# Moving the gates' products of a MoE routing to GpSimd, and its exponentials into one activation

## The chip, the cores and the metric

The kernel runs on one core of one Trainium2 chip. The metric is the device time of one execution in microseconds; the kernel before takes 953.64 us in the median of three runs (951.24 to 955.93). Engines are named as in the profile: PE is TensorE (products; PEld its weight loads), DVE is VectorE, ACT is ScalarE, POOL is GpSimd, and SP issues most DMAs.

## The reference

Three stages follow each other. A delta rule runs over 768 positions of 4 x 8 heads of width 48; its outputs are rows of 384 for 3072 tokens. A mixture of 8 experts sends each token to the expert with the largest logit and multiplies by that token's probability (the gate). A dense block of width 2048 with an ELU ends it.

```python
def _moe_ref(x, expert_emb, tau, w1, w2):
    xn = x / (np.linalg.norm(x, axis=-1, keepdims=True) + 1e-06)
    logits = xn @ en.T / tau
    expert_idx = np.argmax(logits, axis=1)
    probs = np.exp(logits - logits.max(-1, keepdims=True))
    probs /= probs.sum(-1, keepdims=True) + 1e-09
    gate_w = probs[np.arange(N), expert_idx]
    for e in range(E):
        mask = expert_idx == e
        h = np.maximum(x[mask] @ w1[e], 0.0)
        out[mask] = gate_w[mask, None] * (h @ w2[e])
```

Since the largest shifted logit is 0, the gate of a token is 1 over the sum of its exponentials. A positive factor passes through the maximum with zero, so the kernel multiplies the token's row of x by it before the expert.

## The kernel before

**Stages.** The attention stage (up to some 357 us) handles the positions in 12 chunks of 64, each for all heads in two halves. The MoE stage and the dense block come after it and hold most of TensorE's work; they need the routing's tables, which `finish_routing` makes from all routings.

**A pair of chunks needs an inversion.** `invert` builds the inverse T of a small triangular system in 30 steps on GpSimd (L1369: a product into tmp, a subtraction from T, with sizes that grow to 128x128 and shrink again to 128x30). VectorE then transposes T into tile a (L1374, twice), four DMAs carry a into bdT, and TensorE multiplies residuals (rh) by bdT in the recurrence of the next pair. The inversion's steps for one pair run while the recurrence of the pair before it is under way.

**The recurrence.** Its products are on TensorE (L1223). Residuals R are turned into rh by ScalarE (L1100) or VectorE (L1101, L1432), states into Sc (L1470), new values into Zc (L1459); block-diagonal copies bdS, bdZ, bdK, bdKT are made by an engine (L1219, L1220) or by DMA.

**Rows for the MoE.** After each chunk, `to_rows` brings the outputs into token rows (L1519), copies them into one of four slots of tile xt (L1529), the logits' parts into lgp (L1531), and sums the squares into ss (L1533, L1534). Slots are used again by the next pair of chunks; a copy into a slot waits until that slot's scatter has landed.

**A routing.** `route` runs after chunks 1, 3, 5, 7 and 9 for the four tiles in xt (routings 1 to 5 below), and after chunks 10 and 11 for two tiles each. It finds the maximum, each token's place in its expert's queue (di), and the inverse norm rn; then per tile an exponential with scale rn and a sum into gs (L339, on ScalarE); then 1/gs on VectorE (L341, L342); then per tile the gate, a product of 128x384 by a column of gs, on ScalarE (L354) or VectorE (L355); then per tile the scatter, an indirect DMA that GpSimd issues (L348) behind a memset of a single element (L347). After the four scatters GpSimd adds 128 to the tokens' numbers (L359), which waits until all four have landed.

**What sets the order.** In the attention stage nothing is scheduled when the kernel is built: the table `STARTS` holds a due time (units of 10 ns) for every operation, all operations are sorted by it, and each engine gets its own in that order. The table `WAYS` says which engine does an operation that could run on several; its entry "gate" has a digit for each of the 24 gates. Each engine works off its instructions in order; one that waits for a semaphore holds up all behind it on that engine.

## Time and profile before

| | |
|---|---|
| median of 3 runs | 953.64 us (951.24 to 955.93) |
| profiled execution | 954.83 us, span 953.4 us |
| mean granted clock of TensorE over the span | 0.971 |
| PE busy over the span | 834.9 us (88%) |
| DVE | 768.4 us (81%) |
| ACT | 600.4 us (63%) |
| POOL | 464.6 us (49%) |

The page's shares are averages over three stages. The change lies in the attention stage alone, so its windows, its waits and the timelines of single engines around the routings are what to read. A timeline's row gives the start from the beginning of the span, the duration, the engine, the line, the operation with its output and inputs, and in brackets the idle time of the engine just before with what ended it. An engine that sits idle there costs nothing unless a later engine waits for it.

### The profile page before, as it was taken

Reading aid. Unit: us, or ns where it says so; the run is one execution under the profiler, and the core shown is the slowest. Engines: PE = TensorE matmul, PEld = TensorE weight load, DVE = VectorE, ACT = ScalarE, POOL = GpSimd, SP = SyncE. Lnnn points to the kernel's source line nnn. Section 1 sums busy time; section 2 is a strip of 40 time slices with the busy share of each in tenths; the row PEclk is TensorE's granted clock in tenths of the full one; section 3 lists DMA queues with packets and bytes.
Section 4 is the critical chain, followed back from the end, with each engine's and each line's share of the span. In section 5 each row is a group of like instructions: output and inputs, shape, how many; then the busy total and the mean of one; then the engine's idle time right before and its main releaser. Section 6 shows DMA issues by size and latency. Waiting matters only on the chain.

```text
span 953.4 us, 28791 instructions
## 1 busy us (share of the span) xinstructions
PE 834.9 (88%) x11734; PEld 695.9 (73%) x11735; DVE 768.4 (81%) x1563; ACT 600.4 (63%) x1094; POOL 464.6 (49%) x707
## 2 busy tenths in 40 slices
PE   0537888798999877999999999889999999999995
PEld 0426788687888764555556568789999999999995
DVE  6787878778787963988898988998887887787884
ACT  8896779877786954455646636666545455465652
POOL 6564677676776432143433412354345555355452
PEclk9958999999999997999999999999999999999998
DMA  6667865847545418867899263210010100100000
GB/s 207 163 133 204 235 151 114 177 110 136 131 106 140 148 51 267 174 226 196 238 251 212 92 119 98 84 51 18 1 51 18 51 19 18 35 18 18 18 18 18
DMA packets 115365, 107.58 MB, mean 113 GB/s; under 512 B 72889, under 2 KB 100317, under 8 KB 114973
## 3 DMA queue, kind: packets, MB, share of 16 engines
q1 hardware_dynamic: 108649, 82.98, 35.8%
q0 software_dynamic: 6080, 22.05, 7.5%
q8 instruction: 93, 1.52, 0.7%
q10 hardware_dynamic: 500, 0.68, 0.3%
q14 instruction: 43, 0.35, 0.1%
HBM read 74.72 MB, written 19.97 MB: 99 GB/s over the span
## 4 chain that ended last, share of the span: by engine, by line
PE 49%; DVE 7%; issue 2%; DMA 2%; ACT 1%; SPq 0%; POOL 0%; POOLq 0%; DVEq 0%; ACTq 0%
PE pa L662 17%; PE acc L682 15%; PE acc L620 8%; PE pa L601 8%; DMA st<-in_w 2%; DVE w L519 1%; DVE wbl L676 1%; DVE w L518 1%; DVE dal L534 1%; DVE hl L615 0%; DVE wal L668 0%; SPq L471 0%; DVE dbl L534 0%; DVE wah L669 0%; PE pa L573 0%
## 5 line engine op out<-in xcount | busy, mean ns | idle before, releaser
L682 PE MATMUL acc<-dbh,wbl 128*128 128x192 f16 x672 | 165.3, 246 | 1.4 <-DVE wbl L676 1.4
L682 PE MATMUL acc<-dbl,wbh 128*128 128x192 f16 x672 | 165.3, 246 | 0.9 <-DVE dbl L534 0.9
L682 PE MATMUL acc<-dbh,wbh 128*128 128x192 f16 x672 | 165.3, 246 | 0.2 <-DVE y L630 0.2
L662 PE MATMUL pa<-x,dah 128*128 128x256 f16 x1152 | 157.3, 273 | 1.8 <-DVE wal L668 1.4
L682 PEld LDWEIGHTS <-wbh 128*128 128x128 f16 x1344 | 121.9, 98 | 1.5 <-issue 0.3
L662 PEld LDWEIGHTS <-dah 128*128 128x128 f16 x1152 | 111.9, 98 | 14.7 <-issue 2.0
L662 PE MATMUL pa<-x,dal 128*128 128x256 f16 x576 | 94.4, 273 | 0.9 <-DVE dal L534 0.9
L601 PE MATMUL pa<-x,wah 128*128 128x440 f16 (+6 forms) x384 | 77.0, 337 | 1.9 <-DVE hl L615 1.8
L1223 PEld LDWEIGHTS <-bdKT 112*128 112x128 f16 x1680 | 58.3, 101 | 21.0 <-ACT bdKT L1219 6.1
L1223 PEld LDWEIGHTS <-bdK 128*128 128x128 f16 x960 | 40.8, 119 | 42.8 <-ACT rh L1100 18.5
L669 POOL TENSOR_TENSOR wal<-wal 128x256 f32<-128x256 f32 (+1 forms) x67 | 44.8, 669 | 54.9 <-DVE wal L668 31.1
L675 ACT CAST wbh<-wal 128x384 f16<-128x384 f32 (+1 forms) x73 | 41.3, 566 | 44.8 <-PE acc L682 20.4
L682 PEld LDWEIGHTS <-wbl 128*128 128x128 f16 x672 | 65.7, 98 | 3.1 <-DVE wbl L676 2.1
L620 PE MATMUL acc<-hh,wbh 128*128 128x440 f16 (+6 forms) x192 | 64.2, 334 | 2.0 <-DVE y L630 1.1
L620 PE MATMUL acc<-hl,wbh 128*128 128x440 f16 (+6 forms) x192 | 64.1, 334 | 1.2 <-DVE hl L615 1.1
L614 ACT ACTIVATE hh<-pa 128x440 f16<-128x440 f32 (+6 forms) x64 | 31.9, 504 | 52.2 <-PE acc L620 24.8
L620 PE MATMUL acc<-hh,wbl 128*128 128x440 f16 (+6 forms) x192 | 64.0, 334 | 0.0
L675 ACT CAST wbh<-wah 128x384 f16<-128x384 f32 (+1 forms) x82 | 46.0, 562 | 25.8 <-DVE wah L668 11.3
L1223 PEld LDWEIGHTS <-bdL 128*128 128x128 f16 x1536 | 52.0, 97 | 13.7 <-issue 7.1
L662 PEld LDWEIGHTS <-dal 128*128 128x128 f16 x576 | 56.4, 98 | 7.7 <-DVE dal L534 1.2
L665 ACT ACTIVATE wah<-pa 128x512 f32<-128x512 f32 x48 | 28.6, 596 | 48.4 <-PE pa L662 28.0
L601 PEld LDWEIGHTS <-wah 128*128 128x128 f16 x384 | 37.3, 98 | 29.8 <-issue 3.6
(317 smaller groups left out, 2390.5 us busy)
## 6 DMA issues: line engine op xcount, KB each, us to landing
st<-in_w SPq DMA_DIRECT2D x24, 512.0 KB
st<-in_w SPq DMA_DIRECT2D x32, 384.0 KB
kraw<-in_k SPq DMA_DIRECT2D x22, 384.0 KB
w<-in_w_in POOLq DMA_DIRECT2D x12, 512.0 KB, 6.3
w<-in_w_out POOLq DMA_DIRECT2D x16, 384.0 KB, 5.9
xs_scratch<-in_zeros SPq DMA_DIRECT2D x8, 675.5 KB
raw<-in_q SPq DMA_DIRECT2D x12, 448.0 KB
vraw<-in_v SPq DMA_DIRECT2D x12, 384.0 KB
```

What stands on the lines that cost most here:

```text
L518: self.dve(n, lambda m=m, hi=hi: v.scalar_tensor_tensor(out=m, in0=hi, scalar=-0x40000000, in1=m, op0=ALU.bitwise_and, op1=ALU.bitwise_or) ...
L519: self.dve(n, lambda m=m, lo=lo: v.scalar_tensor_tensor(out=m, in0=lo, scalar=29, in1=m, op0=ALU.logical_shift_right, op1=ALU.bitwise_or), ...
L534: self.dve(n, lambda f=f, part=part: v.scalar_tensor_tensor(out=part("l"), in0=f, scalar=sc, in1=part("h"), op0=ALU.mult, op1=ALU.subtract ...
L601: self.nc.tensor.matmul(self.pa[i][:, :n], lhsT=W[w][:, k, c], rhs=x[:, k, y, t0:t0 + n], start=j == 0 and k == 0, stop=j == 2 and k == 2)
L614: self.act(cap, lambda i, hh=hh: nc.scalar.activation(out=hh, in_=self.pa[i][:, :cap], func=AF.Relu), w=[hn], buf=buf)
L620: nc.tensor.matmul(self.acc[d][:, :cap], lhsT=w[:, f, c], rhs=h, start=f == 0 and j == 0, stop=f == 7 and j == 2)
L662: nc.tensor.matmul(o, lhsT=D[w][:, k, c], rhs=x[:, k, y, t0:t0 + 256], start=q + n + k == 0, stop=n + k == 4, skip_group_check=True)
L665: self.act(512, lambda i, t=t: nc.scalar.activation(out=t, in_=self.pa[i], func=AF.Relu, scale=-1.0 / hs), w=[tn], after=wa, buf=buf)
L669: add = lambda o, x, y, op: [(e, n, lambda w=w: w.tensor_tensor(out=o, in0=x, in1=y, op=op)) for e, n, w in (("POOL", o.shape[1] * 128, nc ...
L675: self.op("ghi", ("ACT", n, lambda f=f, fh=fh: nc.scalar.copy(fh, f)), ("DVE", n / 2, lambda f=f, fh=fh: v.tensor_copy(fh, f)), r=[gn + z] ...
L682: nc.tensor.matmul(self.acc[k][:, o:o + HD], lhsT=h[:, u - 1], rhs=D[d][:, p, w - 1], start=p == 0 and n == 0 and o == FIRST[k], stop=p == ...
L1223: self.nc.tensor.matmul(o, lhsT=l, rhs=r, start=st, stop=True, skip_group_check=True)
```

## The change

Two parts. First, the exponentials: VectorE multiplies the shifted logits of all tiles of a routing by rn, ScalarE takes the exponential of all of them in one activation, and VectorE sums over the experts. That makes 7 exponentials of 24, without the accumulator's read behind each; VectorE gets a product and a reduction per routing. Second, a third way for the gate, on GpSimd, and "gate" set to it for the first twenty, which are those of routings 1 to 5; the last four stay as they were.

Empty operations keep the count of table entries as it was. In the table about ten rows change, each exchanging or moving due times of the routing's own operations; one shows the pattern. The gates of routings 1 to 5 keep the due times that they had on ScalarE and VectorE, now among GpSimd's.

```diff
-        for b in tiles:
-            a.act(NE + 140, lambda b=b: nc.scalar.activation(out=self.lgp[:, b, 0], in_=self.lg[:, b], func=AF.Exp, scale=self.rn[:, b:b + 1], accum_out=self.gs[:, b:b + 1]),
-                  r=["rn", "lg", f"lgp{b}"], w=[f"gs{b}"])
-        a.dve(t, lambda: dv.tensor_scalar(out=gs, in0=gs, scalar1=1e-9, scalar2=None, op0=ALU.add), r=names("gs"), w=["gs"])
+        pr = self.lgp[:, part, 0]
+        a.dve(n, lambda: dv.tensor_tensor(out=lg, in0=lg, in1=bc(rn), op=ALU.mult), r=["rn"], w=["lg"])
+        for b in range(t - 2):
+            a.pl.add("NONE", 0.0, lambda: None, w=["lg"])
+        a.act(n, lambda: nc.scalar.activation(out=pr, in_=lg, func=AF.Exp), r=["lg"], w=names("lgp"))
+        a.dve(n + 150, lambda: (dv.tensor_reduce(out=gs, in_=pr, axis=AX.X, op=ALU.add),
+                                dv.tensor_scalar(out=gs, in0=gs, scalar1=1e-9, scalar2=None, op0=ALU.add)), r=names("lgp"), w=["gs"])
...
             a.op("gate", ("ACT", DM + 155, lambda x=x, g=g: nc.scalar.activation(out=x, in_=x, func=AF.Copy, scale=g)),
-                    ("DVE", DM - 130, lambda x=x, g=g: dv.tensor_scalar(out=x, in0=x, scalar1=g, scalar2=None, op0=ALU.mult)), r=["gs"], w=[f"xt{b}"])
+                    ("DVE", DM - 130, lambda x=x, g=g: dv.tensor_scalar(out=x, in0=x, scalar1=g, scalar2=None, op0=ALU.mult)),
+                    ("POOL", DM, lambda x=x, g=g: nc.gpsimd.tensor_scalar(out=x, in0=x, scalar1=g, scalar2=None, op0=ALU.mult)), r=["gs"], w=[f"xt{b}"])
...
-    "gate": "000010010111011011011000",
+    "gate": "222222222222222222221000",
...
-    13905, 13974, 14006, 14051, 14109, 14216, 14138, 14080, 14264, 14292, 14404, 14829, 14576, 14696, 14342, 14430, 14466, 14563, 15217, 10689, 10962, 11031, 11074, 11139, 11206, 11326, 11416, 11480,
+    13905, 13974, 14006, 14051, 14080, 14216, 14138, 14216, 14264, 14292, 14404, 14829, 14576, 14696, 14342, 14430, 14466, 14563, 15217, 10689, 10962, 11031, 11074, 11139, 11206, 11326, 11416, 11480,
```

In the rows below, L359 is the gate and L363 the addition to the tokens' numbers in the changed kernel; further lines stand four higher than before (the scatter is L351, the inversion's steps L1373, the transposition L1378, the residual L1436).

GpSimd at routing 3, before: the inversion's steps of 128x78 on either side, then memsets and scatters (names: tmp, a and T are the inversion's tiles, xt the token rows).

```order
L1369 TENSOR_TENSOR tmp<-a_128,T 128x78
L1369 TENSOR_TENSOR T<-T,tmp 128x3x26
L347 MEMSET gap 1x1
L348 DMA xs_scratch<-xt,di 28672x386
L347 MEMSET gap 1x1
L348 DMA xs_scratch<-xt,di 28672x386
L347 MEMSET gap 1x1
L348 DMA xs_scratch<-xt,di 28672x386
L347 MEMSET gap 1x1
L348 DMA xs_scratch<-xt,di 28672x386
L1369 TENSOR_TENSOR tmp<-a_128,T 128x56
L1369 TENSOR_TENSOR T<-T,tmp 128x2x28
```

The same place in the changed kernel, up to the third scatter; the fourth, and then the inversion's step of 128x56, follow.

```order
L1373 TENSOR_TENSOR tmp<-a_128,T 128x78
L359 TENSOR_SCALAR xt<-xt,gs 128x384
L1373 TENSOR_TENSOR T<-T,tmp 128x3x26
L359 TENSOR_SCALAR xt<-xt,gs 128x384
L350 MEMSET gap 1x1
L351 DMA xs_scratch<-xt,di 28672x386
L359 TENSOR_SCALAR xt<-xt,gs 128x384
L350 MEMSET gap 1x1
L351 DMA xs_scratch<-xt,di 28672x386
L359 TENSOR_SCALAR xt<-xt,gs 128x384
L350 MEMSET gap 1x1
L351 DMA xs_scratch<-xt,di 28672x386
```

Four gates (xt from xt and gs) now stand between the inversion's steps of 128x78 and 128x56, ahead of the scatters.

GpSimd at routing 4, before, from the step of 128x120 to the second half of that of 128x110.

```order
L1369 TENSOR_TENSOR tmp<-a_128,T 128x120
L1369 TENSOR_TENSOR T<-T,tmp 128x6x20
L1369 TENSOR_TENSOR tmp<-a_128,T 128x110
L347 MEMSET gap 1x1
L348 DMA xs_scratch<-xt,di 28672x386
L347 MEMSET gap 1x1
L348 DMA xs_scratch<-xt,di 28672x386
L347 MEMSET gap 1x1
L348 DMA xs_scratch<-xt,di 28672x386
L1369 TENSOR_TENSOR T<-T,tmp 128x5x22
```

And in the changed kernel.

```order
L1373 TENSOR_TENSOR tmp<-a_128,T 128x120
L359 TENSOR_SCALAR xt<-xt,gs 128x384
L1373 TENSOR_TENSOR T<-T,tmp 128x6x20
L1373 TENSOR_TENSOR tmp<-a_128,T 128x110
L350 MEMSET gap 1x1
L351 DMA xs_scratch<-xt,di 28672x386
L359 TENSOR_SCALAR xt<-xt,gs 128x384 x3
L350 MEMSET gap 1x1
L351 DMA xs_scratch<-xt,di 28672x386
L350 MEMSET gap 1x1
L351 DMA xs_scratch<-xt,di 28672x386
L1373 TENSOR_TENSOR T<-T,tmp 128x5x22
```

The first gate stands right behind the step of 128x120, the three others between the first and the second scatter; the inversion's end comes after them.

VectorE at routing 4, before: the new values Zc, the transposition of T into a, the residual rh, a block copy and the states Sc.

```order
L1459 TENSOR_TENSOR Zc<-pw_140,Zc 128x4x96
L1374 STREAM_TRANSPOSE a_128<-T 128x16x16x2 x2
L1432 SCALAR_TENSOR_TENSOR rh_112<-R_136,z_120 128x384
L1219 COPY bdZ<-Zc 64x8x96
L1095 CAST Sc_107<-S_133 128x4x96
L1470 TENSOR_TENSOR Sc_107<-S_133,Sc_107 128x4x96
```

The same in the changed kernel.

```order
L1463 TENSOR_TENSOR Zc<-pw_140,Zc 128x4x96
L1378 STREAM_TRANSPOSE a_128<-T 128x16x16x2 x2
L1436 SCALAR_TENSOR_TENSOR rh_112<-R_136,z_120 128x384
L1223 COPY bdZ<-Zc 64x8x96
L1099 CAST Sc_107<-S_133 128x4x96
L1474 TENSOR_TENSOR Sc_107<-S_133,Sc_107 128x4x96
```

Nothing moved here: the transposition, which waits for the inversion's end on GpSimd, stands ahead of the residual and of the states in both.

## Rows read from the trace of the kernel before

**Rows 1.** Windows of 20 us, 140 to 360: busy us of each engine, their sum.

```profile
sum 220.00, PE 190.02 PEld 170.84 DVE 175.57 ACT 170.27 POOL 139.44; mean PE 17.27 PEld 15.53 DVE 15.96 ACT 15.48 POOL 12.68
```

**Rows 2.** Waits, 140 to 350: engine, line, releaser; us in total, times, longest.

```profile
PE R L1223 <- ACT z L1100: 2.2, 6, 0.6
```

**Rows 3.** Exponentials and gates by source line: ns shortest, median, longest; first and last start.

```profile
L339 ACT ACTIVATE lgp<-lg,rn x24: 284/290/315, 149.2 to 352.5; 128x8 f32<-128x8 f32 x24
L339 ACT ACTIVATION_READ_ACCUMULATOR lgp<-lg,rn x24: 185/190/200, 149.4 to 352.7; 128x1 f32 x24
L354 ACT ACTIVATE xt<-xt,gs x13: 598/612/618, 151.4 to 353.9; 128x384 f32<-128x384 f32 x13
L355 DVE TENSOR_SCALAR xt<-xt,gs x11: 401/410/481, 194.9 to 349.2; 128x384 f32<-128x384 f32 x11
```

**Rows 4.** GpSimd's nearest operations by source line, same columns.

```profile
L514 POOL TENSOR_SCALAR w<-w x3: 1162/1608/1844, 406.2 to 516.0; 128x384 f32<-128x384 f32 x2, 128x512 f32<-128x512 f32 x1
L1107 POOL TENSOR_TENSOR kraw<-kraw,n x14: 827/829/1282, 15.8 to 190.4; 128x384 f32<-128x384 f32 x14
```

**Rows 5.** Timeline of GpSimd: start, us, operation, [idle before <- releaser].

```profile
152.32 1.18 POOL L348 DMA_INDIRECT xs_scratch<-xt,di  x1 [0.98 <-ACT xt L354]
...
156.58 0.97 POOL L348 DMA_INDIRECT xs_scratch<-xt,di  x1 [0.22 <-issue]
...
164.48 1.03 POOL L1369 TENSOR_TENSOR T<-T,tmp 128x30 f16<-128x30 f16 x1
...
210.08 1.84 POOL L1107 TENSOR_TENSOR Kc<-kraw,Kc 128x384 f16<-128x384 f32 x2 [3.48 <-DVE Kc L1289]
...
249.52 1.06 POOL L348 DMA_INDIRECT xs_scratch<-xt,di  x1 [0.43 <-ACT z L1100]
...
256.23 0.43 POOL L1369 TENSOR_TENSOR T<-T,tmp 128x30 f16<-128x30 f16 x1
...
285.82 0.40 POOL L1369 TENSOR_TENSOR tmp<-a,T 128x120 f16<-128x120 f16 x1
...
288.81 1.06 POOL L348 DMA_INDIRECT xs_scratch<-xt,di  x1 [1.62 <-ACT xt L354]
...
298.40 0.24 POOL L1369 TENSOR_TENSOR T<-T,tmp 128x30 f16<-128x30 f16 x1
...
332.50 0.96 POOL L348 DMA_INDIRECT xs_scratch<-xt,di  x1 [0.22 <-DVE wbl L473]
```

**Rows 6.** Timeline of VectorE, same columns.

```profile
161.03 0.54 DVE L1529 COPY xt<-pw 128x384 f32<-128x384 f32 x1
...
168.69 1.31 DVE L1374 STREAM_TRANSPOSE a<-T 128x512 f16<-128x512 f16 x2
...
257.06 1.29 DVE L1374 STREAM_TRANSPOSE a<-T 128x512 f16<-128x512 f16 x2
...
260.68 0.56 DVE L1432 SCALAR_TENSOR_TENSOR rh<-R,z 128x384 f16<-128x384 f32 x1 [0.63 <-PE R L1223]
...
287.64 0.18 DVE L342 RECIPROCAL gs<-gs 128x4 f32<-128x4 f32 x1
...
298.68 1.31 DVE L1374 STREAM_TRANSPOSE a<-T 128x512 f16<-128x512 f16 x2
...
300.44 0.56 DVE L1432 SCALAR_TENSOR_TENSOR rh<-R,z 128x384 f16<-128x384 f32 x1 [0.46 <-PE R L1223]
```

**Rows 7.** Timeline of TensorE's products.

```profile
261.84 0.36 PE L1223 MATMUL pw<-rh,bdT 128*128 128x48 f16 x8
...
301.62 0.36 PE L1223 MATMUL pw<-rh,bdT 128*128 128x48 f16 x8
```

**Rows 8.** The scatter's line: time from the DMA to its landing.

```profile
DMA to landing us min/median/max: 2.7/3.2/5.8
```

**Rows 9.** Timeline of TensorE's weight loads.

```profile
176.88 0.47 PEld L1223 LDWEIGHTS <-bdT 128*128 128x128 f16 x16 [0.47 <-DMA bdT<-a]
```

**Rows 10.** Timeline of ScalarE.

```profile
337.87 0.48 ACT L1529 COPY xt<-pw 128x384 f32<-128x384 f32 x1 [0.69 <-PE pw L1519]
```

10 rows, old and new, of the table STARTS are left out of this document.

## The prediction

> **What bounds the kernel now.** I read the windows by 20 us first: the change lies wholly between 149 and 356 us, in the attention stage, and there TensorE is busy 190.02 of 220 us while no other engine is above 175.57 [rows 1]. So the end of the stage is set by TensorE's products and by what TensorE has to wait for. The MoE stage starts from the finished routing tables, hence a stage that ends d later moves the whole rest by d, and I price every edit by what TensorE loses or gets back.
>
> Next I read the waits. TensorE's largest wait for ScalarE, the engine that the change relieves, comes to 2.2 us in six places [rows 2]; the other groups of that kind are smaller. That caps the gain: a shorter ScalarE queue gives back at most some 5 us, though it loses far more work than that.
>
> Last I read GpSimd in order of time. At 20 us to the window it looks half free, but its work around a routing is one queue: the steps of the inversion T, the routing's four scatters, then the rest of T, all in the table's order. VectorE's transposition of T (L1374) stands at a fixed place in VectorE's order and waits for T's last step; the residuals of the recurrence (L1432, rh), which TensorE multiplies next, stand behind it.
>
> **The exponentials.** 24 activations at 290 ns, each with a read of its accumulator at 190 ns [rows 3], take 11.5 us of ScalarE. Seven activations of 128x32 or 128x16 remain; the nearest row is that of 128x8 at 290, so about 7 x 0.3 = 2.1. ScalarE gets 9.4 us. VectorE gets seven products and seven sums; its small operations of this kind take 0.18 (the reciprocal at 287.64) [rows 6], so some 14 x 0.2 = 2.8 are added. For one routing the path from the norm to gs is 4 x 0.48 before, and 0.2 + 0.3 + 0.2 now with two hand-overs more: between 0 and 1 us shorter, and I take nothing for the last routing, whose four gates are as before.
>
> **The gates leave ScalarE and VectorE.** Of the first twenty, ten were on ScalarE at 612 ns and ten on VectorE at 410 [rows 3]: 6.1 and 4.1 us. With the exponentials ScalarE is relieved of 15.5 us, VectorE of 1.3. Of the cap of 5 us I take 1.2 (0.5 to 3): most of those waits are not at a routing.
>
> **The gates arrive on GpSimd.** No row shows a product of 128x384 by a column of scalars there. The nearest row is a tensor_scalar of the same shape and type, L514: 1162 ns at its shortest, 1608 in the middle; a product of two such tensors, L1107, takes 829 [rows 4]. I take 1.16, and with the hand-over 1.2 per gate; the ends are 0.88 and 1.65. Twenty of them are 24 us (18 to 33) of new work in a queue on which four inversions and twenty scatters depend. Now each routing in turn; "T" is the inversion's last step.
>
> *Routing 3.* Four gates add 4.8, and the first scatter's wait of 0.43 goes: +4.4. T ended at 256.66 and the transposition began at 257.06 [rows 5, 6]; now T ends at 261.0, so the transposition is 4.0 late. Behind it rh began at 260.68 after 0.63 of idleness, so rh is 3.4 late, and TensorE, which read it at 261.84 with 0.6 to spare [rows 7], loses 2.7 (1.5 to 4.5).
>
> *Routing 4.* The first gate stands right behind the step of 128x120, which ends at 286.2 [rows 5], and waits there for gs, ready at 287.82 [rows 6]: 1.6 of waiting takes the place of the 1.62 in front of the scatter at 288.81 [rows 5]. The net is the four gates, +4.8. Here T ended at 298.64 and the transposition began at 298.68: no slack at all. rh (300.44, 0.46 of idleness) is 4.3 late, TensorE wanted it at 301.62, 0.62 after it was there [rows 6, 7]: 3.7 lost, and 0.5 more because the states (Sc) that TensorE reads right after stand behind rh on VectorE. I take 4.2 (2.4 to 6).
>
> *Routing 1.* T is hidden: it ended at 165.5, the transposition began at 168.69. But the fourth scatter moves from 156.58 by 4.8 less the 0.98 that the first one waited for a gate, to 160.4 [rows 5]; it lands 2.7 to 3.2 later [rows 8], at 163.1 to 163.6, and VectorE's copy into that slot of xt (L1529, at 161.03) must wait for it: 2.1 to 2.6 late. VectorE is nearly without idle time from there to the transposition, so that and the DMA of bdT go late too, and for bdT TensorE's weight load already waits 0.47 at 176.88 [rows 9]. I take 1.8 (0 to 4).
>
> *Routing 2.* GpSimd sits idle 3.48 at 210.08, before T's last step [rows 5]; the four gates' 4.8, less what the first scatter had waited for its gate, overfill it by 1 at most. I take 0.4 (0 to 1.5).
>
> *Routing 5.* No inversion is left. The third scatter moves from 332.50 to about 336.9 [rows 5], lands at 339.6 to 340.1, and ScalarE's copy into its slot began at 337.87 [rows 10]: 1.7 (0.4 to 4).
>
> The sum: 1.8 + 0.4 + 2.7 + 4.2 + 1.7 = 10.8 lost, 1.2 gained. After a loss the engines that were late catch up in TensorE's own idle time, 30 of 220 us [rows 1]; I take 2.2 back, a fifth. Net +7.4. On the profiled execution (954.83) that gives 962.2; it lies 1.2 above the median of the runs, and on the median, 953.64, the forecast is **961.0**. With every term at its low end (gates at 0.88) the sum is 0.3 + 0 + 1.5 + 2.4 + 0.4 = 4.6 lost, about +2, 956; at the high end 20 lost, about +15, 969.
>
> **Where a page of the Trainium skill speaks.** In rows 4 the same shape takes 1.16 us or more. The Trainium skill, "GPSIMD Engine Reference", section 4.1 Engine selection, says that an elementwise operation with one input runs at about line rate there; with the 1.2 GHz of its section 1, 384 elements would be 0.32 us of streaming, by estimate 0.5 with a fixed part, and the sum by it about +0.5. The rows of L514 speak against it.
>
> **The rivals.**
>
> *The gate is cheap.* If a gate takes half of what L514 shows, 0.55 to 0.6, four are 2.4. Routing 4 is then 2.4 late at T, 1.3 on TensorE; routing 3 is 2.0 late at T, 0.7 on TensorE; routing 1's scatter lands at 160.9, before 161.03; routings 2 and 5 lose nothing that counts. 2.0 lost, 1.2 gained, a little caught up: 953 to 955, not slower. For it: the product of two tensors takes 0.83, though it reads more. Against it: the one operation of the same kind and shape takes 1.16. The price decides: below 0.8 us the loss no longer shows in a measurement. Chance 0.22. By the page's rule it would be this case.
>
> *Gates and VectorE hold each other up.* L514's middle is 1608 against 1162 [rows 4]: something stretches it. With all gates at 1.6 the terms are the high ends: +12 to +15, 966 to 969. Chance 0.14. The Trainium skill, "SBUF — State Buffer", section SBUF: two separate sides, says that VectorE and GpSimd share a pair of ports under an exclusive lock, so that the second to come waits for a whole instruction; L514's spread agrees.
>
> *ScalarE was the bound of the routing's neighbourhood.* If the exponentials' and gates' places on ScalarE did hold up the chain, up to 5 us come back; for 949 or less the losses above must be hidden too, by T's transposition not being wanted. Rows 6 and 7 speak against it: rh is read within 0.6 us of its end. 949 to 951. Chance 0.10.
>
> **How the numbers follow.** The forecast, a gate of 0.9 to 1.4 us with the delays through T, has 0.54 and spans 956 to 966. An outcome counts as faster or slower beyond 0.5%, 4.8 us, about what a measurement of this kernel can tell from no change: slower is over 958.4. Of the forecast's 0.54 I put 0.44 there and 0.10 below; the stretched gates add 0.14: slower 0.58. Same: 0.10, 0.20 of the cheap gates, 0.05 of the ScalarE case: 0.35. Faster: 0.02 and 0.05. The range, 953.5 to 967.5, takes in the forecast, the upper part of the cheap gates and the lower part of the stretched ones.
>
> **What would show it.** In the profile after: a GpSimd group of twenty tensor_scalars of 128x384 with a mean of 1.1 to 1.3 us; the transposition behind routing 4 waiting for T by 3 to 5 us, behind routing 3 by 2 to 4; TensorE's waits for rh from VectorE up by 5 or more; the copies into xt behind routings 1 and 5 waiting for a scatter by 1 to 3. Waits of TensorE for ScalarE should hardly change. A gate mean under 0.7, or transpositions that wait no more than before, would make the prediction wrong; so would losses after routing 4 that are gone by 340 us, since then the catching up is larger than a fifth.

## The result, and the profile after

The changed kernel takes 968.74 us in the median of five runs (967.60 to 969.85), the kernel before beside it 953.52 (951.24 to 955.93): a ratio of 1.0148, interval 1.0121 to 1.0175. So it is slower, as forecast, but by 15.2 us where 7.4 were forecast, and 1.2 above the range. The profiled execution took 968.56, its span is 967.1 against 953.4. Further series of runs then put the sign itself in question, and the experiments below are mostly about that.

What answers to [rows 1], the sum over the eleven windows of 20 us, 140 to 360:

```profile
sum 220.00, PE 185.87 PEld 167.41 DVE 167.32 ACT 152.95 POOL 156.39; mean PE 16.90 PEld 15.22 DVE 15.21 ACT 13.90 POOL 14.22
```

ScalarE lost 17.3 us of work, GpSimd gained 17.0, and TensorE did 4.2 us less in the same time. (The windows are fixed, so in the slower kernel they end earlier in the work; the twenty gates alone are 25.7 us.) The gate, which answers to [rows 4], by its source line (ns shortest, median, longest; first and last start):

```profile
L359 POOL TENSOR_SCALAR xt<-xt,gs x20: 1237/1256/1561, 146.8 to 344.8; 128x384 f32<-128x384 f32 x20
```

To see where the time went one row serves as a milestone: every routing begins with the same product of TensorE (L322, the ranks in a queue). By source line, before and after, with its first and last start:

```profile
L322 PE MATMUL pw<-oh,tri x7: 169/176/176, 147.6 to 351.7; 128*128 128x32 bf16 x5, 128*128 128x16 bf16 x2
```

```profile
L322 PE MATMUL pw<-oh,tri x7: 169/176/177, 143.2 to 364.4; 128*128 128x32 bf16 x5, 128*128 128x16 bf16 x2
```

The changed kernel came to the first routing 4.4 us earlier, ahead of every changed instruction; from the first to the last routing it took 221.2 us instead of 204.1, 17.1 more (17.0 by the unrounded starts); behind the last one it took 1.0 more. That is the 13.7 by which the spans differ. The earlier start is chance as far as the traces tell: over all 19 traces, of both kernels and of the experiments, the first of these products starts between 141.7 and 148.6 us. From one L322 to the next, us ("r1" is the stretch from routing 1 to routing 2, as in the forecast), with some kernels of the experiments that are spoken of further down:

| kernel (profiled execution) | r1 | r2 | r3 | r4 | r5 | sum |
|---|---|---|---|---|---|---|
| before | 45.2 | 54.1 | 37.1 | 36.6 | 26.5 | 199.5 |
| after | 48.9 | 54.6 | 40.2 | 44.9 | 27.9 | 216.5 |
| before, once more (b1) | 50.8 | 56.0 | 39.2 | 40.5 | 31.6 | 218.0 |
| after, once more (a2) | 47.7 | 53.8 | 39.9 | 43.1 | 28.1 | 212.6 |
| exponentials alone (e1) | 51.0 | 55.8 | 41.9 | 41.7 | 32.8 | 223.3 |
| after, scatters in a row (f2) | 47.2 | 57.6 | 39.5 | 46.2 | 29.8 | 220.2 |
| before, scatters 2 us apart (h1, first series) | 46.1 | 53.3 | 39.3 | 43.7 | 27.7 | 210.0 |
| before, scatters 2 us apart (h1, second series) | 46.0 | 53.1 | 38.3 | 39.0 | 27.7 | 204.1 |
| before, same work, scatters in a row (h2) | 49.3 | 57.7 | 41.0 | 41.0 | 29.0 | 218.0 |

In the first pair the losses are 3.7, 0.5, 3.1, 8.3 and 1.4. Routing 4, the largest, on GpSimd, after (start, duration, [idle before <- releaser]):

```profile
290.84 1.25 POOL L359 TENSOR_SCALAR xt<-xt,gs 128x384 f32<-128x384 f32 x1 [1.08 <-DVE gs L345]
...
294.21 4.02 POOL L359 TENSOR_SCALAR xt<-xt,gs 128x384 f32<-128x384 f32 x3
...
302.64 1.61 POOL L1330 TENSOR_TENSOR vraw<-vraw,n 128x384 f32<-128x384 f32 x2
...
306.76 0.24 POOL L1373 TENSOR_TENSOR T<-T,tmp 128x30 f16<-128x30 f16 x1
...
308.73 3.04 POOL L1342 TENSOR_TENSOR Qc<-raw,Qc 112x256 f16<-112x256 f32 x4
```

The inversion's end comes late, as forecast: the transposition waits for it, which answers to [rows 6].

```profile
307.04 1.31 DVE L1378 STREAM_TRANSPOSE a<-T 128x512 f16<-128x512 f16 x2 [5.49 <-POOL T L1373]
308.27 0.54 DVE L1436 SCALAR_TENSOR_TENSOR rh<-R,z 128x384 f16<-128x384 f32 x1
308.83 3.16 DVE L1223 COPY bdZ<-Zc 64x768 f16<-64x768 f16 x1
```

But TensorE stops earlier, for something that the forecast did not name. GpSimd also scales vraw (L1330), the next pair's values, and ScalarE starts R from it. ScalarE, after:

```profile
303.51 0.48 ACT L1407 COPY R<-vraw 128x384 f32<-128x384 f32 x1 [5.25 <-POOL vraw L1330]
303.92 0.48 ACT L1104 ACTIVATE rh<-R 128x384 f16<-128x384 f32 x1
```

And TensorE, after, which answers to [rows 7]:

```profile
304.46 0.48 PE L1227 MATMUL pw<-rh,bdT 128*128 128x48 f16 x8 [3.13 <-ACT rh L1104]
304.76 1.46 PE L1227 MATMUL pw<-Qc,bdS 112*128 112x64 f16 x24
306.03 1.47 PE L1227 MATMUL pw<-Ac,bdZ 128*128 128x64 f16 x24
...
308.92 1.41 PE L1227 MATMUL pw<-z,idh 128*128 128x384 f16 x4
310.17 0.36 PE L1227 MATMUL pw<-rh,bdT 128*128 128x48 f16 x8
...
312.63 0.56 PE L1227 MATMUL R<-Sc,bdKT 112*128 112x48 f16 x16 [1.40 <-DVE Sc L1099]
```

Before, the three groups of 24, 24 and 4 products took 0.86, 0.87 and 0.81; the first of them:

```profile
298.37 0.86 PE L1223 MATMUL pw<-Qc,bdS 112*128 112x64 f16 x24
```

The windows of 2 us show why (the third number from the right is the granted clock):

```profile
302.00:304.00 2.00, 0.00 (x0) 0.00 (x0) 0.00 (x0) 0.49 (x2) 1.98 (x4) 0.83 0.26 99
304.00:306.00 2.00, 1.54 (x32) 1.54 (x32) 0.00 (x0) 1.27 (x3) 1.69 (x6) 0.50 0.06 12
306.00:308.00 2.00, 2.00 (x46) 2.00 (x44) 0.96 (x2) 1.75 (x1) 1.64 (x6) 0.50 0.17 37
308.00:310.00 2.00, 2.00 (x32) 1.50 (x30) 1.97 (x3) 1.86 (x6) 2.00 (x3) 0.50 0.20 35
310.00:312.00 2.00, 1.24 (x34) 0.97 (x33) 1.99 (x1) 0.58 (x1) 1.77 (x3) 0.96 0.65 98
```

TensorE stood idle for 3.1 us, and then worked at 0.50, the lower of its two levels (1.2 GHz), until about 310. Against the same products before (offset 2.95 on entry), it is 6.3 late behind the wait for vraw, 8.5 behind the slow stretch, 10.1 behind the wait for Sc, and 11.25 at the end of r4: 3.3 + 2.3 + 1.6 + 1.1. The last 1.1 is a wait put down to issue, 1.67 at 324.46 where 0.48 stood before.

The wait for Sc comes from the copy of 3.16 us above. Before, this copy took 0.36:

```profile
301.03 0.36 DVE L1219 COPY bdZ<-Zc 64x768 f16<-64x768 f16 x1
```

In the changed kernel it ran beside four products of GpSimd, from 308.73 to 311.77, and ended 0.2 after them. The Trainium skill, "SBUF — State Buffer", section SBUF: two separate sides, says that GpSimd and VectorE, the latter in a two-port mode or with two inputs in SBUF, hold a shared pair of ports each for a whole instruction while the other is blocked. The 3.16, as long as all four products, is of that kind, and so is 3.17 in f2 and in h1's first trace; but in a1 and a2 the copy beside the same products took 0.95 and 0.98, some 0.6 longer than 0.36 and less than one of these products; which mode the copy ran in no trace tells.

Two more traces of the changed kernel (a1 and a2, spoken of below) do not repeat all of this. There r4 takes 42.7 and 43.1 us, 6.1 and 6.5 above the first trace of before. R waits 3.99 and 3.96 for vraw, but TensorE does not wait for what is made from it: it loses time in several waits of 0.4 to 1.5 us, the longest (1.51) for the rh that VectorE makes, and the granted clock stays at 1.00. T's transposition waits only 2.09 and 2.06 (a2's row below). So TensorE's 3.13 for vraw, the 2.3 of the lower clock and most of the 1.6 belong to the one execution above; that routing 4 costs more than 4.2 us is in all three.

```profile
306.89 1.31 DVE L1378 STREAM_TRANSPOSE a<-T 128x512 f16<-128x512 f16 x2 [2.06 <-POOL T L1373]
```

### The profile page after: what moved, and what is told of

Same layout as the page of the kernel before. It is cut to its first block, busy times and chain, and to the rows that moved or that the text cites. A ratio compares the mean times of both kernels' runs of the same rounds, so it can differ in the third digit from the quotient of the medians.

```text
span 967.1 us, 28767 instructions
## 1 busy us (share of the span) xinstructions
PE 841.4 (87%) x11734; PEld 700.7 (72%) x11735; DVE 771.8 (80%) x1567; ACT 590.7 (61%) x1043; POOL 487.8 (50%) x727
## 4 chain that ended last, share of the span: by engine, by line
PE 48%; DVE 6%; issue 2%; DMA 2%; ACT 1%; POOL 0%; POOLq 0%; SPq 0%; DVEq 0%; ACTq 0%
PE pa L666 17%; PE acc L686 15%; PE acc L624 8%; PE pa L605 8%; DMA st<-in_w 2%; DVE w L523 1%; DVE wbl L680 1%; DVE w L522 1%; DMA xr<-xs_scratch 1%; DVE dal L538 1%; DVE hl L619 0%; DVE wal L672 0%; DVE dbl L538 0%; DVE wah L673 0%; PE pa L577 0%
## 5 line engine op out<-in xcount | busy, mean ns | idle before, releaser
L1227 PEld LDWEIGHTS <-bdK 128*128 128x128 f16 x960 | 40.7, 119 | 39.2 <-ACT rh L1104 17.8
L679 ACT CAST wbh<-wal 128x384 f16<-128x384 f32 (+1 forms) x73 | 41.3, 565 | 45.0 <-PE acc L686 22.2
L669 ACT ACTIVATE wah<-pa 128x512 f32<-128x512 f32 x48 | 28.6, 596 | 48.4 <-PE pa L666 28.0
```

Source lines behind the costliest of these rows:

```text
L669: self.act(512, lambda i, t=t: nc.scalar.activation(out=t, in_=self.pa[i], func=AF.Relu, scale=-1.0 / hs), w=[tn], after=wa, buf=buf)
L679: self.op("ghi", ("ACT", n, lambda f=f, fh=fh: nc.scalar.copy(fh, f)), ("DVE", n / 2, lambda f=f, fh=fh: v.tensor_copy(fh, f)), r=[gn + z] ...
L1227: self.nc.tensor.matmul(o, lhsT=l, rhs=r, start=st, stop=True, skip_group_check=True)
```

## The experiments

The experiments were run in five series: e1 to e4; b1 and a1; f1 to f4; a2, g1, g3 and h1; and h1 again, h2 and h3. Each series ran the kernel before beside the others. It is the base of the ratios, and it took 974.67, 973.48, 973.43, 974.47 and 972.19 us in the five, on four chips (the second and the third on the same one; 968.0 to 979.1 in all): 20 above its 953.5 beside the first run of the change. So the first two experiments, planned as halves of a known difference, met another difference.

**The two parts apart.** e1 has the single exponentials and the old gates, by the digits below; e2 is the kernel before with the gate's third way and the new digits.

```diff
-    "gate": "222222222222222222221000",
+    "gate": "000010010111011011011000",
```

> The changed kernel with the gates back on ScalarE and VectorE by the old digits; only the exponentials in one activation remain. If the loss of 15 us is GpSimd's queue behind the gates, this kernel is at 950 to 954. If the new products and sums on VectorE, or the moved table entries of the routing, cost a part of it, it is above 956.

> The kernel before with the first twenty gates on GpSimd and the exponentials as they were, 24 on ScalarE. If the gates alone make the loss: 967 to 971, and the transposition behind routing 4 waits for the inversion by 5 us or more, as in the changed kernel. If the two parts cost about the same each: 960 to 963.

e1: 977.36, ratio 1.0028 (1.0004 to 1.0052). e2: 969.12, ratio 0.9944 (0.9916 to 0.9972). The exponentials alone give nothing (if anything they cost 0.3%), and the gates, which should cost, seem to gain 5.5 us.

**Both kernels once more**, unchanged: b1 is the kernel before, a1 and a2 are the changed one.

> The kernel before itself, unchanged, for a second profile: on the chip of the first four experiments it took 974.7 us where it had taken 953.5 beside the changed kernel. If TensorE there lacks its instructions in time (idle with nothing to wait for, at 16 KB instruction packets that come late), its idle time put down to issue between 140 and 380 us is up by some 10 us or more over the first profile's. If it is other engines that are late, the named waits (DMA, ScalarE, VectorE) are up instead.

> The changed kernel itself, beside the kernel before on this chip. The kernels with gates on GpSimd took 966 to 971 on the chip of the first four experiments, the one without 977, the kernel before 974.7. If the chip decides the sign: 968 to 972, not slower than the kernel before where that takes 972 or more. If the first comparison holds on every chip: 1.5% above the kernel before.

> The changed kernel once more, beside the kernel before. If the chip makes the sign: where the kernel before takes about 973, the changed one takes 966 to 970 (ratio 0.991 to 0.996); where it takes about 954, the changed one takes 967 to 970 (ratio 1.014). If it is chance from run to run and not the chip, the ratio should land anywhere between 0.99 and 1.015.

b1: 971.95, ratio 0.9993 (0.9969 to 1.0017). a1: 966.62, ratio 0.9917 (0.9883 to 0.9951). a2, on another chip: 964.71, ratio 0.9899 (0.9845 to 0.9952). So the changed kernel takes 965 to 969 everywhere, and it is the kernel before that takes either 954 or 973. Where it takes 973, the change is faster by about 1%. The table shows that b1's excess of 18.5 us over the first trace lies between the first routing and the last (it came to the first one 3.4 us earlier). Here is routing 2 of b1, first GpSimd's scatters, then TensorE, then ScalarE:

```profile
197.38 1.05 POOL L348 DMA_INDIRECT xs_scratch<-xt,di  x1 [0.82 <-ACT xt L354]
198.73 0.97 POOL L348 DMA_INDIRECT xs_scratch<-xt,di  x1 [0.21 <-DVE Ac L1265]
200.00 0.96 POOL L348 DMA_INDIRECT xs_scratch<-xt,di  x1 [0.22 <-issue]
```

```profile
198.27 0.68 PE L1223 MATMUL pw<-Qc,bdS 112*128 112x64 f16 x13
199.41 0.32 PE L1223 MATMUL pw<-Qc,bdS 112*128 112x64 f16 x5 [0.46 <-issue]
200.14 0.28 PE L1223 MATMUL pw<-Qc,bdS 112*128 112x64 f16 x4 [0.42 <-issue]
200.86 0.22 PE L1223 MATMUL pw<-Qc,bdS 112*128 112x64 f16 x2 [0.43 <-issue]
```

```profile
201.64 0.48 ACT L1095 CAST Sc<-S 128x384 f16<-128x384 f32 x1 [3.56 <-PE pw L1223]
```

The scatters start 1.3 us apart. While they run, TensorE needs 2.8 us for a group of 24 products that took 0.86 in the first trace, waiting for nothing that the profile shows ("issue"), and ScalarE waits behind it. At routing 5 it is worse; TensorE and then ScalarE of b1 ("remote" too names no engine of this core):

```profile
344.21 0.48 PE L1223 MATMUL R<-z,ip 128*128 128x384 f16 x1 [4.01 <-issue]
```

```profile
343.67 0.49 ACT L1100 ACTIVATE z<-pw 128x384 f16<-128x384 f32 x1 [4.20 <-remote]
```

The scatters there start at 338.69, 340.15, 341.42 and 342.69. In the first trace the scatters of routing 2 start just as close, at 195.22, 196.58, 197.85 and 199.25, and the group of 24 beside them takes 0.86:

```profile
196.12 0.86 PE L1223 MATMUL pw<-Qc,bdS 112*128 112x64 f16 x24
```

What the expectation of b1 looked for is there in part: between 140 and 380 us the waits put down to issue rise from 1.1 to 8.1 us ahead of TensorE's products in the recurrence (10 or more were looked for), and from 19.0 to 33.1 ahead of its weight loads, which overlap with products. Late transfers of instructions, which it suspected, do not show: from 140 to 345 us the instruction queue's packets of 16 KB, 38 in the first trace and 35 in b1, take 1.3% of the DMA engines' time in both.

The silences cost a second time, through the clock. At routing 2 TensorE is busy 0.51 of the 2 us from 200 to 202, and from 204 to 206 its granted clock is 0.50. Over the eleven windows of 20 us from 140 to 360 the granted clock has a mean of 0.945 in b1 and of 0.982 in the first trace, by estimate some 8 of the 18.5 us (0.037 of 220). One of b1's windows, where the first trace shows 1.00 (the third number from the right):

```profile
140.00:160.00 20.00, 15.15 (x370) 12.77 (x367) 11.96 (x32) 15.37 (x36) 13.93 (x35) 0.91 0.39 89
```

In the changed kernel a gate stands ahead of many scatters. In its first trace eight of the fifteen distances within routings 1 to 5 are 2.5 to 5.3 us, the other seven 1.3 to 1.6. That gave a new theory: scatters in a row starve TensorE, on the chips of these series, and the change gains there because its gates space them. The rival: something else in the gates' move helps.

**The distance of the scatters.** f2 is the changed kernel with four gates and then four scatters in a row (due times; one row of the table is shown). f1 is the kernel before with a pass of 128x384 on GpSimd, as long as a gate, ahead of each scatter of routings 1 to 5, h1 the same with 128x128, and h2 has the passes of h1 all ahead of one scatter of the routing, so that the others still follow each other directly. The passes multiply by 1.

```diff
-    17510, 17675, 17588, 17786, 17817, 17868, 17939, 17969, 18022, 18077, 18106, 18193, 18179, 18315, 18315, 18564, 18599, 19114, 19177, 18743, 19044, 18682, 18778, 18778, 18911, 19675, 14706, 15180,
+    17510, 17675, 17588, 17786, 17817, 17868, 17939, 17969, 18022, 18077, 18106, 18193, 18179, 18315, 18315, 18564, 18599, 19114, 19177, 18743, 19117, 18682, 19115, 18778, 19116, 19675, 14706, 15180,
```

```diff
         def scatter(b):
+            if not last:
+                nc.gpsimd.tensor_scalar(out=xt[:, b, :128], in0=xt[:, b, :128], scalar1=1.0, scalar2=None, op0=ALU.mult)
```

```diff
         def scatter(b):
+            for _ in range(4 if not last and b == tiles[0] else 0):
+                nc.gpsimd.tensor_scalar(out=xt[:, b, :128], in0=xt[:, b, :128], scalar1=1.0, scalar2=None, op0=ALU.mult)
```

> The changed kernel with the four gates of each of the routings 1 to 5 in a row and the four scatters in a row behind them; GpSimd does the same work. If scatters in a row starve TensorE on these chips: 973 to 982 and the silences of 2 to 4 us are back. If the spacing does not matter: 965 to 969.

> The kernel before, gates and exponentials as they were, with one more operation of 128x384 on GpSimd ahead of each of the first twenty scatters: a pass over the token rows that multiplies by one, so GpSimd's queue is about that of the changed kernel. On the chips of the experiments the kernel before takes 972 to 975 and TensorE falls silent for 2 to 4 us at routings whose scatters follow each other directly. If the spacing of the scatters is what the change gains there, and GpSimd's queue what it costs: 966 to 972, and no such silence. If it is the relief of ScalarE and VectorE that gains: 980 or more, since here nothing is relieved. On a chip where the kernel before takes 953: 965 to 970 by both.

> The kernel before, with a short GpSimd pass of 128x128 ahead of each of the first twenty scatters; it leaves the values as they are and only spaces the scatters, by an estimated 0.45 us each. The passes of 128x384 spaced them by 1.3 and cost GpSimd as much as the gates. If spacing is what relieves TensorE: the stretches in which it trickles without a wait shrink from about 7 us to 2 and the time is 4 to 8 below the kernel before where that takes 973. If the spacing has to be the full 1.3: no change, within 2.

> The kernel before with short passes of 128x128 once more. If the spacing of the scatters relieves TensorE: 957 to 961 where the kernel before takes 970 to 975, and about 952 to 957 where the kernel before takes 954, since nothing starves there. If 958.2 was chance: within 3 of the kernel before.

> The same passes, but all four of a routing ahead of its first scatter, so that GpSimd's work is the same and the scatters follow each other as directly as in the kernel before. If the spacing is what counts: TensorE trickles as in the kernel before and the time is that of the kernel before or up to 3 above, 970 to 977. If something else about the passes helps (a shifted start of the scatters, other work moved): 957 to 962 as with spacing.

f2: 973.99, ratio 1.0012 (0.9983 to 1.0041); the whole gain of the changed kernel is gone. f1: 970.06, ratio 0.9974 (0.9947 to 1.0000). h1: 958.16, ratio 0.9837 (0.9785 to 0.9889), and in a second series 962.23, ratio 0.9891 (0.9862 to 0.9920): 10 to 16 us faster, by nothing but added work. h2: 971.21, ratio 0.9992 (0.9966 to 1.0019): the same added work without the distance gains nothing. Routing 2 in the second run of h1, GpSimd and TensorE:

```profile
195.32 1.21 POOL L350 DMA_INDIRECT xs_scratch<-xt,di  x1 [0.25 <-POOL gap L349]
196.56 0.68 POOL L348 TENSOR_SCALAR xt<-xt 128x128 f32<-128x128 f32 x1
197.53 1.03 POOL L350 DMA_INDIRECT xs_scratch<-xt,di  x1 [0.24 <-POOL gap L349]
198.59 0.68 POOL L348 TENSOR_SCALAR xt<-xt 128x128 f32<-128x128 f32 x1
199.55 1.08 POOL L350 DMA_INDIRECT xs_scratch<-xt,di  x1 [0.24 <-POOL gap L349]
```

```profile
195.27 0.86 PE L1225 MATMUL pw<-Qc,bdS 112*128 112x64 f16 x24
```

The scatters are 2.2 and 2.0 us apart, the group of 24 takes 0.86 again, and while the four scatters run TensorE waits for issue 0.15 at most. The granted clock's mean over the eleven windows is 0.976. In h2, with three of the scatters 1.3 apart, it trickles, and the clock's mean is 0.936:

```profile
201.66 0.32 PE L1225 MATMUL pw<-Qc,bdS 112*128 112x64 f16 x5 [0.43 <-issue]
202.40 0.25 PE L1225 MATMUL pw<-Qc,bdS 112*128 112x64 f16 x3 [0.41 <-issue]
203.11 0.19 PE L1225 MATMUL pw<-Qc,bdS 112*128 112x64 f16 x1 [0.46 <-issue]
```

So the distance is what counts on those chips. f1 has the distance too, 2.5 us or more at every scatter, but its passes hold GpSimd as long as the gates do, and its stretches in the table's measure (49.0, 54.3, 41.3, 43.2, 28.6) are close to those of the changed kernel. By the ratios it lies 0.8 to 1.4% above h1. That this is the price of GpSimd's work, twice h1's per pass, is likely but not shown: f4, below, takes 6.6 us of such work away and gains nothing. f1 also lies 3.4 us above a1 on the same chip (ratio 0.9974 against 0.9917, intervals that just overlap), with the gates' work still on ScalarE and VectorE; so that their relief is worth something is not ruled out. A kernel without the scatters of these routings, which would show TensorE with none beside it, was not run.

**The exponentials without the starved stretches.** h3 is e1 with the passes of h1.

> The single exponentials and the gates on ScalarE and VectorE as before, with the short passes between the scatters. If the exponentials are worth something once TensorE is not starved: 953 to 957, 1 to 4 below the kernel with passes alone. If ScalarE's relief gives nothing, as the forecast's 1.2 would: the same within 2, 956 to 961.

h3: 960.04, ratio 0.9865 (0.9834 to 0.9896), beside h1's 0.9891 in the same series and 0.9837 in the other. The exponentials are worth nothing that can be measured here either.

**Routing 4.** e3 gives its gates back to ScalarE and VectorE, e4 puts GpSimd's product of vraw ahead of three gates, f3 has only routing 4's gates on GpSimd.

```diff
-    "gate": "222222222222222222221000",
+    "gate": "222222222222011022221000",
```

```diff
-    30328, 30440, 30482, 27264, 28240, 26517, 26976, 28718, 28944, 29449, 29593, 29675, 29758, 29876, 29958, 30000, 30091, 30186, 30261, 30261, 30364, 30471, 30555, 30593, 30643, 30750, 30784, 30817,
+    30328, 30440, 30482, 27264, 27640, 26517, 26976, 28718, 28944, 29449, 29593, 29675, 29758, 29876, 29958, 30000, 30091, 30186, 30261, 30261, 30364, 30471, 30555, 30593, 30643, 30750, 30784, 30817,
```

```diff
-    "gate": "222222222222222222221000",
+    "gate": "000010010111222211011000",
```

> The changed kernel with the four gates of routing 4 back on ScalarE and VectorE. Aligned by TensorE's instructions, the traces of before and after drift apart by some 8 us between 285 and 325 us, where I had priced 4.2. If that stretch is the part that was mis-sized: 960 to 962. If the forecast's term was right and the excess lies elsewhere: 964 to 966.

> The changed kernel with one operation moved in GpSimd's order: at routing 4 the product of the new values vraw (two instructions, 1.6 us) goes from behind the gates and scatters to ahead of the second gate. In the trace of after ScalarE's copy of vraw into R waits 5.25 us for it, and TensorE then 3.13 for rh. If that chain, which the prediction did not price, is what TensorE lost first at routing 4: 3 to 5 us back, 964 to 966. If the transposition's wait for T (5.49 us of VectorE) sets the loss anyway: within 1 of 968.7.

> The exponentials in one activation, and of the gates only routing 4's on GpSimd. Counterpart to the kernel with routing 4 back (965.8, against 966.6 for the changed kernel on another chip). On a chip where the kernel before takes 953: 6 to 8 us above it, if routing 4's stretch in the first pair of traces is the gates' doing. Where it takes 973: if the gates' queue costs routing 4 more than the spacing gives, 975 to 980; if the two cancel there, 970 to 974.

e3: 965.82, ratio 0.9914 (0.9889 to 0.9939). e4: 971.11, ratio 0.9972 (0.9949 to 0.9994). f3: 976.53, ratio 1.0040 (1.0013 to 1.0067). The changed kernel was not in e3's and e4's series, so they are compared with it by the ratios (0.9917 for a1, 0.9899 for a2). e3's r4 takes 40.3 us, 2.8 less than a2's, though its scatters are in a row again; in the whole nothing of that is left, and the 965.8 lies where its expectation put an excess that is elsewhere than at routing 4. e4 gains nothing and is rather slower, and its waits between 286 and 316 us (engine, line, releaser; total, times, longest) say why:

```profile
DVE a L1378 <- POOL T L1373: 4.4, 1, 4.4
...
PE pw L1227 <- DVE rh L1436: 3.3, 1, 3.3
```

With vraw early TensorE waits 3.3 us for rh behind the transposition instead. That is the path of the forecast; in the first trace of the changed kernel the wait for vraw stood in front of it and hid it. f3 leaves routings 1, 2, 3 and 5 as they were in e1 and is no faster than e1 (ratio 1.0040 against 1.0028); its r4 is 43.9 us, e1's 41.7.

**The gate's price, and the slow copy.** f4 makes the gate a product of two tensors, gs spread over the row; g1 is f4 with e3's change; g3 puts the copy that took 3.16 us on ScalarE (one digit of the table "bd", 1 to 2).

```diff
-                    ("POOL", DM, lambda x=x, g=g: nc.gpsimd.tensor_scalar(out=x, in0=x, scalar1=g, scalar2=None, op0=ALU.mult)), r=["gs"], w=[f"xt{b}"])
+                    ("POOL", DM, lambda x=x, g=g: nc.gpsimd.tensor_tensor(out=x, in0=x, in1=g.to_broadcast([128, DM]), op=ALU.mult)), r=["gs"], w=[f"xt{b}"])
```

> The changed kernel with GpSimd's gate as a product of two tensors, the second a broadcast column, which the row of 829 ns says is a third cheaper than the 1256 of the tensor_scalar. If the gates' price sets the loss through GpSimd's queue: 20 x 0.4 = 8 us less on GpSimd, 3 to 6 us less in all. If the queue does not bind: within 1 of the changed kernel. If a broadcast operand costs more than it saves, the mean of the group shows it.

> The changed kernel with the gates as products of two tensors (834 ns in place of 1256) and routing 4's gates back on ScalarE and VectorE. Each part alone gave about -3 on the changed kernel. If both act on different places they add: 960 to 963. If the scatters of routing 4, which then follow each other directly, starve TensorE for some 3 us, what routing 4 gives is eaten: 965 to 967.

> The changed kernel with one block copy (bdZ of routing 4, which took 3.16 us on VectorE beside GpSimd's product) on ScalarE. If GpSimd's work holds up VectorE's copy and TensorE's 1.4 us wait for Sc comes from that: the copy takes under 0.7 on ScalarE, TensorE's wait there goes below 0.4, total 1 to 2 below the changed kernel in this call. If the copy is slow for another reason (its operands), ScalarE's takes 2 or more as well and nothing is gained.

The gates of f4 by source line:

```profile
L359 POOL TENSOR_TENSOR xt<-xt,gs x20: 817/834/1542, 152.2 to 344.3; 128x384 f32<-128x384 f32 x20
```

f4: 965.75, ratio 0.9921 (0.9888 to 0.9955), the same as a1's 0.9917, though the gates cost GpSimd 6.6 us less (a mean of 0.96 instead of 1.29); by its expectation that says that GpSimd's queue does not bind there, though the cheaper gates also bring the scatters closer together. g1: 965.32 beside a2's 964.71 in the same series, so the two changes give nothing together either; its routing 4 has stretches of "remote" again. g3: 967.32; the copy takes 0.83 on ScalarE and TensorE's wait for Sc is gone there, but the time is not below a2's. The collision costs 1.4 us at its place in the first trace, 0.5 in a2, and nothing that can be seen in the whole.

## Why the prediction was wrong

**The price of a gate** held: 1256 ns in the median, a mean of 1291, where 1.16 and 1.2 with the hand-over were taken and 1.1 to 1.3 was the sign to look for. The Trainium skill's rule of line rate for one input ("GPSIMD Engine Reference", section 4.1 Engine selection), 0.5 us by the forecast's estimate from it, does not agree with the trace's 1256 ns.

**Routings 2, 3 and 5** held: 0.5, 3.1 and 1.4 against 0.4, 2.7 and 1.7. Routing 3 went by the forecast's steps, the transposition waiting 3.19 for T (forecast 2 to 4) and TensorE 1.25 for rh and then 1.19 for the DMA of bdS. At routing 5 ScalarE's copy into xt waits 2.56 for its scatter, which answers to [rows 10].

**Routing 4 is the step that failed**: 4.2 forecast, 8.3 measured. The path was wrong. The loss was to reach TensorE through T's transposition and the rh that VectorE makes, and TensorE's waits for rh from VectorE were to rise by 5 us or more; between 140 and 350 us they rose from 4.6 to 5.5, while those for rh from ScalarE rose from 0.8 to 3.5. The delay of T itself was near the forecast (5.49 of waiting against 3 to 5), and in e4 it cost TensorE 3.3. But the list of what stands behind the gates on GpSimd was not complete: the product into vraw stands there too, and its reader R is wanted earlier than T. It came in time before:

```profile
295.26 0.82 POOL L1326 TENSOR_TENSOR vraw<-vraw,n 128x384 f32<-128x384 f32 x1
```

(GpSimd before; ScalarE copied it at 296.75.) And the sum priced a wait at its own length. What follows a wait of 3 us was not in it: 2.3 us at the lower clock, and 1.6 for a copy of VectorE that ran beside GpSimd's products and the states behind it. The forecast's 0.5 for the states was that term, too small. This account stands on the first pair of traces. In a1 and a2 R waits for vraw too, but TensorE's wait behind it, the lower clock and the long copy are missing, and r4 costs 6.1 to 6.5 there in smaller waits. No run with one edit gives the 8.3 back (e3 and e4, run where the kernel before takes 974, do not), so which of routing 4's waits sets its cost from one execution to the next stays open.

**Routing 1** went by the forecast's path and was mis-sized: 1.8 forecast, 3.7 measured. VectorE's copy into xt waits 3.40 us, where 1 to 3 was the sign. Its row names L1523, but GpSimd's addition, which waits until all four scatters have landed, starts at the same time, so we read the wait as one for the landing. Behind that copy stands the block copy bdS, for which TensorE waits:

```profile
161.22 0.56 DVE L1533 COPY xt<-pw 128x384 f32<-128x384 f32 x1 [3.40 <-PE pw L1523]
```

```profile
161.28 0.24 POOL L363 TENSOR_SCALAR xt<-xt 128x4 int32<-128x4 int32 x1 [1.56 <-DMA xs_scratch<-xt,di]
```

```profile
162.69 0.92 PE L1227 MATMUL pw<-Qc,bdS 112*128 112x64 f16 x24 [1.55 <-DVE bdS L1223]
```

The windows from 164 to 170 then show a granted clock of 0.50, where before they show 1.00. With it, 24 products take 1.47 instead of 0.87.

**ScalarE's relief** was to give 1.2, and the catching up 2.2. Neither shows in the first pair. (Its cap of 5 was read a little low: TensorE's waits for ScalarE sum to 6.1 us between 140 and 350. And the low end of its sum takes 0.3 for routing 1, whose own range begins at 0. Nothing hangs on either.) TensorE's waits for z from ScalarE went from 2.2 to 1.4 [rows 2], and e1 and h3 find no gain in the exponentials; whether the gates' leaving gains something was not tested by itself. Nothing was caught up: the traces were 11.25 us apart behind routing 4, 12.7 at the last routing and 13.7 at the end of the span.

So the terms came to 17.0 instead of 10.8 less 3.4. The miss of the time is smaller by luck: the changed kernel's trace was 4.4 us ahead before its first changed instruction, which is no term of the sum. The rival of stretched gates gave the right time for another reason, since the gates' mean was 1.29 and not 1.6.

**What the forecast could not see** is that the kernel before has two times. Its trace showed scatters 1.3 us apart with TensorE at full pace beside them. In the later series the same scatters starve TensorE, and b1's five stretches are 18.5 us longer; the change takes a good part of that away and, as we read it, puts its own cost in its place: the stretches come to 216.5 and 212.6 in after and a2, between before's 199.5 and b1's 218.0. So it is slower by 1.5% in the first comparison and faster by 0.8 to 1.0% in the later ones. h1 against h2 shows that the distance of the scatters does it on those chips. Why the first pair's execution is free of it stays open. The chip is one possibility, since the first one's was not told and four others agree among themselves, but the series differ in time as well; and nothing in the trace names what TensorE's instructions wait for in those stretches. The forecast's sign, slower, was right in the first pair and wrong in both later series that had the changed kernel.

## What to carry to other kernels

When work is put into an engine's queue, list everything behind it there, with the first reader of each, and not only the chain that one is looking at; the earliest reader may set the loss. Look at the granted clock behind every wait of TensorE of some 3 us, and price the products there at the lower level; here they took 2.3 us on top of 3.1. And where an engine issues indirect transfers in a row, try a short piece of work between them first: 20 passes of 0.6 us gained 10 to 16 us in two series, and in the one that had the changed kernel beside them they beat it by 6.6. Before trusting a sign of 1%, run the kernel before in more than one series: here it took 953.5 us in one and 972 to 975 in five.

## What the runs showed of the hardware

- Four indirect transfers that start 1.3 us apart on GpSimd slow TensorE's instruction stream to a trickle, 2.8 us for 24 products instead of 0.86, with gaps of up to 4.0 us without any releaser (b1), and the granted clock behind them falls to 0.50; 2.0 us apart they do not (h1). The traces of e1, b1 and h2, from three chips, show the trickle; the first pair's do not.
- On GpSimd the product of 128x384 by a column took 1256 ns, the same product with the column spread as a second tensor 834 (medians; means 1291 and 964).
- A copy of VectorE of 64x768 in f16 took 3.16 us, against 0.36, beside four products of GpSimd (3.17 in f2 and in h1's first trace, 0.95 and 0.98 in a1 and a2); on ScalarE it took 0.83.
- Behind idle times of 1.55 and 3.13 us TensorE's granted clock was 0.50 (1.2 GHz) for some 6 us each time; behind one of 1.48 in the first trace of before, and one of 1.51 in a2, it stayed at 1.00.
